# Block products in the second group, weight sums on GpSimd, state products between blocks: a fused scan and feed-forward kernel on one core

**Chip, cores, metric.** One core of one Trainium2 chip. The metric is the device time of one execution in microseconds. All times compared here are of fast runs; a core alone has no second die to compare with, so a run counts as slow only where it is over 1.5% above the fastest of its kernel.

## The reference, cut to what matters

```python
# state-space scan: batch 4, 8 heads, 768 steps, head 32, state 16, chunks of 32
for c in range(nc):
    cum = np.cumsum(log_a_chunk, axis=-1)
    L = np.exp(cum[:, :, :, None] - cum[:, :, None, :]) * causal
    y = einsum((Cc @ Bc^T) * L, xc) + (Cc @ state) * exp(cum)     # ... cut
    state = exp(sum(log_a_chunk)) * state + sum(Bc x xc * decay)  # ... cut
# feed-forward on all 3072 tokens, 256 -> 2048 -> 256
h = x @ w_in
g = h * (1.0 / (1.0 + np.exp(-1.702 * h)))
return g @ w_out
```

All is float32. The kernel takes chunks of 128 steps and the tokens in six groups of 512; a group is two pairs of chunks. While group g goes through the two big products, the state work of group g+1 is done.

## The kernel before

The feed-forward has 8 blocks of hidden units a group. A block's product, cut into 2 x 2 parts, takes 8 part products in the plain way or 7 by the known trick of mixing the parts with sums beforehand and afterwards. Mixing the weights costs 32 sums, once for the whole kernel:

```python
def mix_in(n):                                   # n = 0..3, for blocks 2n, 2n+1 of the first product
    ...
    for o, u, v, op in ((s1, a21, a22, ALU.add), (s2, s1, a11, ALU.subtract),
                        (s3, a11, a21, ALU.subtract), (s4, a12, s2, ALU.subtract)):
        nc.vector.tensor_tensor(out=o, in0=u, in1=v, op=op)   # 128 x 256, float32
    ...
def mix_w(n): ...                                # the same for the second product's weights
def mix_y(g): ...                                # three sums that mix the group's input yT
```

`hidden(g, f)` is half a plain block: two matmuls of 512 columns (a matmul leaves two records in these traces: the 16 plain blocks of four matmuls are 128 records of L660). `first(g, j, i)` is one of the seven products of block j; the letters D, T, S in the order strings are the additions (VectorE) and Silu calls (ScalarE) that follow. `product(g, j)` is a block of the second product, by seven already. The state work of a pair p: `decay` (VectorE scans, L352, and Be, L397), `turn` (transposes), `advance` (TensorE A, then VectorE S: L582, L589), `score` (TensorE cb, L539), `weigh` (VectorE multiplies L by cb in PSUM, L550), `finish` (TensorE y, L607 and L616, then ScalarE copies into yT). The first group is all plain, groups 3 to 6 all by seven. The second group stands between them with an order of its own, plain in the first product:

```python
for step in "H0 H1 H2 H3 H4 P0 H5 P1 H6 P2 H7 P3 P4 P5".split():
    j = int(step[1:])
    if step[0] == "H":
        hidden(1, 2 * j)
        hidden(1, 2 * j + 1)
    else:
        product(1, j)
    for do in after.get(step, []):     # state work and sums, listed by step  ... cut
        do()
for g in range(2, NG):                 # the loop of the later groups  ... cut
```

Of the kernel before, what the change touches and what calls it, by code (L numbers as in the profile page):

```python
# [16 lines left out]
P = 128  # L17
# [18 lines left out]
def kernel(  # L36
# [444 lines left out]
    def turn(p):  # L481
        turn_only(p)
        since_start(p)
# [61 lines left out]
    def weigh(p, ks=(slice(0, 2),)):  # L545

        L, cb = Ls[p], st[p]["cb"]
        Lv = L.rearrange("p k r q i -> p k r (q i)")
        for k in ks:
            nc.vector.tensor_tensor(out=Lv[:, k], in0=Lv[:, k],  # L550
                                    in1=cb.rearrange("p r k e -> p k r e")[:, k], op=ALU.mult)
# [7 lines left out]
    def gain(p):  # L559
        b, c = divmod(2 * p, NC)  # L560
        Be = BE.pop(p)
        nk = 1 if c + 2 == NC else 2
        A = bank(f"A{p}")[:, :2 * Q * D].rearrange("p (k e) -> p k e", k=2)
        for k in range(nk):
            for r in range(R):
                heads = slice(Q * r, Q * r + Q)
                nc.tensor.matmul(out=A[32 * r:32 * r + 32, k],  # L567
                                 lhsT=Be[:, k, heads].rearrange("p h n -> p (h n)"),
                                 rhs=rx[p][:, k, heads].rearrange("p h d -> p (h d)"),
                                 start=True, stop=True, tile_position=(0, 32 * r),  # L570
                                 skip_group_check=True)
        increment[p] = A
# [20 lines left out]
    def finish(p, late=False):  # L593
        for part_of in finish_parts(p, late):
            part_of()
# [73 lines left out]
    def mix_in(n):  # L669

        t = wide.tile([P, PN], FP32, tag=("m", "p2")[n % 2], name=f"mi{n}").rearrange(
            "p (j s e) -> p j s e", j=2, s=4)
        w = w_in[:, :, 4 * n * P:4 * (n + 1) * P].rearrange(
            "p k (j i e) -> p k j i e", j=2, i=2)
        a11, a12, a21, a22 = w[:, 0, :, 0], w[:, 1, :, 0], w[:, 0, :, 1], w[:, 1, :, 1]
        s1, s2, s3, s4 = (t[:, :, i] for i in range(4))
        for o, u, v, op in ((s1, a21, a22, ALU.add), (s2, s1, a11, ALU.subtract),
                            (s3, a11, a21, ALU.subtract), (s4, a12, s2, ALU.subtract)):
            nc.vector.tensor_tensor(out=o, in0=u, in1=v, op=op)
        for k in range(2):  # L680
            mixed_in[2 * n + k] = t[:, k]

# [88 lines left out]
    def mix_w(n):  # L771

        if n % 2 == 0:
            mixed_w["tile"] = words(f"mw{n}").bitcast(FP32).rearrange(
                "p (n j s e) -> p n j s e", n=2, j=2, s=4)
        t = mixed_w["tile"][:, n % 2]
        w = w_out[:, 4 * n:4 * n + 4].rearrange("p (j i) (c e) -> p j i c e", i=2, c=2)
        a11, a12, a21, a22 = w[:, :, 0, 0], w[:, :, 1, 0], w[:, :, 0, 1], w[:, :, 1, 1]
        s1, s2, s3, s4 = (t[:, :, i] for i in range(4))
        for o, u, v, op in ((s1, a21, a22, ALU.add), (s2, s1, a11, ALU.subtract),  # L780
                            (s3, a11, a21, ALU.subtract), (s4, a12, s2, ALU.subtract)):
            nc.vector.tensor_tensor(out=o, in0=u, in1=v, op=op)
        for k in range(2):
            mixed_w[2 * n + k] = t[:, k]

# [173 lines left out]
    def at(places, i, *work):  # L959
        places.setdefault(i, []).extend(work)  # L960
# [24 lines left out]
    at(in_project[0], 7, lambda: turn(PG + 1))  # L985
    at(in_project[0], 9, lambda: narrow(9))
    at(in_project[0], 10, lambda: advance(PG + 1), lambda: scores(PG + 1))
    at(in_project[0], 14, lambda: finish(PG + 1))
    for i in range(4):
        at(in_project[0], 14, lambda i=i: mix_in(i))  # L990
    for k in range(PG):
        at(in_project[0], 8 + k, lambda k=k: load(2 * PG + k))
    for k, i in enumerate((9, 11, 13, 15)):
        at(in_project[0], i, lambda k=k: spread(2 * CG + k))


    after = {}
    n, p = 2 * PG, 3 * PG

    def late(p):  # L1000
        gain(p)
        keep(p)
        score(p)
        weigh(p)

    at(after, "H0", lambda: decay(2 * CG), lambda: decay(2 * CG + 1), lambda: turn(n))
    at(after, "H1", lambda: late(n), lambda: decay(2 * CG + 2), lambda: decay(2 * CG + 3),
       lambda: turn(n + 1))
    at(after, "H3", lambda: finish(n), lambda: load(p + 1), lambda: late(n + 1))
    at(after, "H4", lambda: finish(n + 1))  # L1010
    for k, i in enumerate(("H4", "P0", "P2", "P5")):
        at(after, i, lambda k=k: mix_w(k))
    for j in range(NF // 2):
        at(after, f"P{min(j - 1, 5)}" if j else "H4", lambda j=j: mix_g(1, j))
    for k in range(CG):
        at(after, f"P{k}", lambda k=k: decay(3 * CG + k))
        at(after, "H1" if k < 2 else "H3", lambda k=k: spread(3 * CG + k))
    at(after, "P3", lambda: clip_rows(2), lambda: decay_rows(2), lambda: turn(p))
    at(after, "P4", lambda: mix_y(2), lambda: advance(p), lambda: turn(p + 1))
    at(after, "P5", lambda: advance(p + 1))  # L1020
    assert [b for b in range(NB) if 3 * CG <= b * NC < 4 * CG] == [2]


    for f in range(NF):
# [1 line left out]
        for do in in_hidden[0].get(f, []):  # L1026
            do()
    project_all(0, in_project[0])
    load(p)
    spread_rows(2)  # L1030
    for step in "H0 H1 H2 H3 H4 P0 H5 P1 H6 P2 H7 P3 P4 P5".split():
        j = int(step[1:])
        if step[0] == "H":
            hidden(1, 2 * j)
            hidden(1, 2 * j + 1)
        else:
            product(1, j)
        for do in after.get(step, []):
            do()

    def run(g, steps, products=(), **do):

# [12 lines left out]
    def seven(g, j):  # L1055
        return [(g, j, (i,)) for i in ORDER]

    for g in range(2, NG):
        n, p = (g + 1) * PG, (g + 2) * PG
        more, most = g + 1 < NG, g + 2 < NG  # L1060
        chunks = list(range((g + 2) * CG, (g + 3) * CG)) if most else []
        rows = [b for b in range(NB) if most and (g + 2) * CG <= b * NC < (g + 3) * CG]
        if most:
            load(p)
            for c in chunks[:2]:
                spread(c)
            for b in rows:
                spread_rows(b)
        run(g, "0.1 P P 0.6 P P 0.7 P 0.5 P 0.2 P 0.D", seven(g - 1, 6))
        run(g, "1.1 0.S P 0.4 P P 1.6 P 0.3 0.T M P P 1.7 P 1.5 1.2 1.D C", seven(g - 1, 7),  # L1070
            M=lambda: mix_g(g, 0), C=lambda: combine(g - 1))
        if more:
            a, b = finish_parts(n), finish_parts(n + 1)
            run(g, "2.1 1.S 1.4 1.3 2.6 2.5 2.2 2.7 1.T s1 2.D 2.S w1 2.4 give 2.3 3.1 2.T s2 w2 3.6 "
                "y1 3.7 y2 y3 3.5 3.2 3.D", s1=lambda: score(n), w1=lambda: weigh(n), give=lambda: give(g - 1),
                s2=lambda: score(n + 1), w2=lambda: weigh(n + 1), y1=a[0], y2=a[1], y3=a[2])
            if most:
                load(p + 1)
                for c in chunks[2:]:
                    spread(c)  # L1080
            run(g, "P P 3.S 3.4 P P 3.3 3.T P P P M", seven(g, 0), M=lambda: mix_g(g, 1))
            for r in rows:
                clip_rows(r)
                decay_rows(r)
            run(g, "4.1 y1 4.6 4.5 y2 4.7 4.2 y3 4.D M", y1=b[0], y2=b[1], y3=b[2],
                M=lambda: mix_g(g, 2))
            if most:
                decay(chunks[0])
        else:
            run(g, "2.1 1.S 1.4 1.3 2.6 2.5 2.2 2.7 1.T 2.D 3.1 2.S 2.4 3.5 3.6 2.3 3.2 3.7 2.T 3.D M",  # L1090
                M=lambda: mix_g(g, 1))
        for j in range(5 if more else 4, NF // 2):
            h = "{1}.1 {0}.S P {0}.4 P {1}.6 P {0}.3 P {1}.7 {0}.T P {1}.5 P {1}.2 P {1}.D M".format(j - 1, j)
            run(g, h, seven(g, j - 4), M=lambda: mix_g(g, j - 2))
            if most:
                decay(chunks[j - 4])
        k = NF // 2 - 1
        run(g, f"P {k}.S P {k}.4 P P {k}.3 {k}.T P P P", seven(g, 4))
        if not more:
            give(g - 1)  # L1100
            for j in range(k - 1, k + 1):
                mix_g(g, j)
            break
        mix_g(g, 6)
        if most:
            turn(p)
        mix_y(g + 1)
        run(g, "P P A P T P P P P B", seven(g, 5),
            **{"A": lambda: most and advance(p), "T": lambda: most and turn(p + 1),
               "B": lambda: most and advance(p + 1)})  # L1110
        mix_g(g, 7)
# [33 lines left out]
```

## Time and profile before

| | before |
|---|---|
| median of the first runs | 383.5 us |
| span of the profiled run | 383.8 us |
| TensorE busy | 97% |
| chain of waits on TensorE | 95% |

The stage in which the change lies can be cut out by two instructions that all versions have: the scores of the second group's second pair (cb), and the first product X of group 3. From the first to the second I call it the stage. These are their rows in the TensorE timeline of the kernel before (start, length, engine, line, output and inputs, shapes, records):

```profile
79.38 1.15 PE L539 MATMUL cb<-CT,BT 32*128 32x256 f32 x16
...
147.75 0.70 PE L717 MATMUL X<-yT,w_in 128*128 128x256 f32 x2
```

The stage takes 147.75 - 79.38 = 68.37 us. From group 3's start it is another 231.7 us to the start of TensorE's last record. I call this the tail; in the traces below it is the same to 0.03 us, with two exceptions that are named where they come up.

The chain of waits before, by engine:

```profile
PE 95%; DVE 2%; DMA 1%; ACT 1%; issue 1%; ACTq 0%; DVEq 0%
```

### The profile page before, as it was taken

The numbers are of one execution on the slowest core, as the hardware profiler recorded it, in microseconds if no ns is written. First come the engines' busy times: TensorE is split into PE (matmuls) and PEld (weight loads), VectorE is DVE, ScalarE is ACT, GpSimd is POOL, SyncE is SP. The second block draws the span as 40 slices with busy tenths as digits, with TensorE's granted clock in tenths as the row PEclk, the third lists the DMA queues.
The fourth block names the chain that finished last, engine by engine and source line by source line (L and its number), as shares of the span: only waits on it lengthen the run. The fifth ranks groups of instructions, "written<-read, shape, count | busy, mean of one in ns | idle before, by whom it ended". The sixth has DMA issues, their size and how long they took to land.

```text
span 383.8 us, 5725 instructions
## 1 busy us (share of the span) xinstructions
PE 373.2 (97%) x2258; PEld 281.1 (73%) x2258; DVE 267.7 (70%) x438; ACT 152.0 (40%) x337; POOL 11.7 (3%) x34
## 2 busy tenths in 40 slices
PE   7979999999999999999999999999999999999995
PEld 3544447886556678877888867888877888888884
DVE  4589998999879968567787564879383446454353
ACT  3658836401432122553333453333453432453330
POOL 5210000000000010000000000000000000000000
PEclk9999999999999999999999999999999999999999
DMA  9998949442967110068200045000010000000011
GB/s 150 235 252 199 242 149 178 86 168 62 194 102 161 73 43 0 0 110 167 81 30 0 2 84 138 0 0 2 0 56 2 0 0 3 0 0 2 0 56 55
DMA packets 85794, 29.56 MB, mean 77 GB/s; under 512 B 75720, under 2 KB 79240, under 8 KB 85768
## 3 DMA queue, kind: packets, MB, share of 16 engines
q1 hardware_dynamic: 83592, 28.94, 32.4%
q10 hardware_dynamic: 2176, 0.26, 0.5%
q8 instruction: 18, 0.29, 0.3%
q14 instruction: 8, 0.07, 0.1%
HBM read 25.95 MB, written 3.24 MB: 76 GB/s over the span
## 4 chain that ended last, share of the span: by engine, by line
PE 95%; DVE 2%; DMA 1%; ACT 1%; issue 1%; ACTq 0%; DVEq 0%
PE acc L814 32%; PE X L717 16%; PE h L660 14%; PE Y L727 11%; PE o L757 7%; PE cb L539 3%; PE y L616 3%; PE ab L460 2%; PE tp L496 2%; PE y L607 2%; PE oT L848 1%; PE A L567 1%; DMA az<-in_a_dram 1%; DVE L L550 1%; ACT yT L638 0%
## 5 line engine op out<-in xcount | busy, mean ns | idle before, releaser
L814 PE MATMUL acc<-mg,mw 128*128 128x256 f32 x240 | 65.3, 379 | 0.0
L660 PE MATMUL h<-yT,w_in 128*128 128x512 f32 x128 | 56.9, 595 | 0.0
L722 ACT ACTIVATE ac<-X 128x256 f32<-128x256 f32 x64 | 24.6, 384 | 77.0 <-PE X L717 77.0
L831 DVE TENSOR_TENSOR gT<-Y,ac 128x512 f32<-128x512 f32 x32 | 22.1, 692 | 46.4 <-PE Y L727 44.4
L814 PEld LDWEIGHTS acc<-mg,mw 128*128 128x128 f32 x240 | 45.4, 190 | 6.1
L694 ACT ACTIVATE gT<-gT 128x512 f32<-128x512 f32 x64 | 33.3, 520 | 30.5 <-DVE gT L831 30.5
L660 PEld LDWEIGHTS h<-yT,w_in 128*128 128x128 f32 x128 | 23.9, 190 | 27.6 <-issue 25.7
L814 PE MATMUL acc<-gT,w_out 128*128 128x256 f32 x160 | 43.8, 380 | 0.0
L352 DVE TENSOR_TENSOR_SCAN L<-a,idents 128x1024 f32<-128x1024 f32 x18 | 41.1, 2283 | 0.0
L717 PE MATMUL X<-my,mi 128*128 128x256 f32 x128 | 39.3, 389 | 0.1
L663 ACT ACTIVATE gT<-h 128x512 f32<-128x512 f32 x32 | 19.0, 595 | 41.5 <-PE h L660 41.2
L814 PEld LDWEIGHTS acc<-gT,w_out 128*128 128x128 f32 x160 | 29.9, 190 | 5.3 <-issue 1.4
L831 DVE TENSOR_TENSOR gT<-Y,b 128x256 f32<-128x256 f32 x32 | 13.5, 421 | 29.0 <-PE Y L727 29.0
L550 DVE TENSOR_TENSOR L<-L,cb 128x2048 f32<-128x2048 f32 (+1 forms) x13 | 27.6, 2122 | 3.8 <-PE cb L539 3.7
L757 PE MATMUL o<-w_out,gT 128*128 128x256 f32 x128 | 29.3, 383 | 0.0
L685 DVE TENSOR_TENSOR mg<-gT 128x512 f32<-128x512 f32 x40 | 27.3, 684 | 1.9 <-ACT gT L694 1.9
L717 PEld LDWEIGHTS X<-my,mi 128*128 128x128 f32 x128 | 23.3, 190 | 5.3 <-ACT gT L694 1.0
L757 PEld LDWEIGHTS o<-w_out,gT 128*128 128x128 f32 x128 | 23.8, 190 | 4.1 <-issue 0.7
L814 PE MATMUL acc<-gT,mw 128*128 128x256 f32 x80 | 23.7, 382 | 0.0
L814 PE MATMUL acc<-mg,w_out 128*128 128x256 f32 x80 | 23.5, 379 | 0.0
L717 PE MATMUL X<-yT,w_in 128*128 128x256 f32 x64 | 19.7, 389 | 0.9 <-ACT yT L638 0.9
L722 ACT ACTIVATE b<-X 128x256 f32<-128x256 f32 x32 | 12.3, 384 | 19.8 <-PE X L717 19.7
(134 smaller groups left out, 522.2 us busy)
## 6 DMA issues: line engine op xcount, KB each, us to landing
a<-scratch SPq DMA_DIRECT2D x18, 512.0 KB, 5.6
bits<-in_moe_w_out_dram SPq DMA_DIRECT2D x4, 1024.0 KB, 7.1
x<-in_x_dram SPq DMA_DIRECT2D x24, 128.0 KB, 3.4
out_dram<-ob SPq DMA_DIRECT2D x11, 256.0 KB, 2.2
bits<-in_moe_w_in_dram SPq DMA_DIRECT2D x4, 512.0 KB
bits<-in_moe_w_in_dram SPq DMA_DIRECT2D x2, 1024.0 KB
b<-in_B_dram SPq DMA_DIRECT2D x24, 64.0 KB, 3.9
c<-in_C_dram SPq DMA_DIRECT2D x22, 64.0 KB, 2.7
```

The lines of the kernel that those rows point to most:

```text
L352: nc.vector.tensor_tensor_scan(out=Ls[p][:, k].rearrange("p r q i -> p (r q i)"), data0=ra[n], data1=idents.rearrange("p h i -> p (h i)"), ...
L550: nc.vector.tensor_tensor(out=Lv[:, k], in0=Lv[:, k], in1=cb.rearrange("p r k e -> p k r e")[:, k], op=ALU.mult)
L660: nc.tensor.matmul(out=h, lhsT=w_in[:, k, f * P:(f + 1) * P], rhs=yT[g][:, k], start=(k == 0), stop=(k == NK - 1))
L663: nc.scalar.activation(gT[g, j][:, i], h, AF.Silu, scale=GELU_SCALE)
L685: nc.vector.tensor_tensor(out=t[:, 0:2], in0=B[:, :, 1], in1=B[:, 0], op=ALU.subtract)
L694: nc.scalar.activation(o, i, AF.Silu, scale=GELU_SCALE)
L717: nc.tensor.matmul(out=s["X"], lhsT=lhsT, rhs=rhs, start=i == "1", stop=i == "4", skip_group_check=True)
L722: nc.scalar.activation(copy, s["X"], AF.Copy)
L727: nc.tensor.matmul(out=o, lhsT=lhsT, rhs=rhs, start=s.pop("new", False), stop=i != "5", skip_group_check=True)
L757: nc.tensor.matmul(out=o[k // 2][:, k % 2], lhsT=gT[g, f // 2][:, f % 2, k * P:(k + 1) * P], rhs=w_out[:, f], start=(f == 0 and k % 2 == 0 ...
L814: nc.tensor.matmul(out=acc[g][0][i], lhsT=lhsT, rhs=rhs, start=(j == 0 and i in (0, 2, 5, 6)), stop=(j == NF // 2 - 1), skip_group_check=True)
L831: nc.vector.tensor_tensor(out=o, in0=v, in1=w, op=ALU.add)
```

## The change

Its intent: give the second group the cheaper seven products from block 3 on, take the 32 weight sums off VectorE, the second busiest engine, and lay the state's output products between running blocks as the later groups do. The diff in full:

```diff
--- before.py
+++ after.py
@@ -676,7 +676,7 @@
         s1, s2, s3, s4 = (t[:, :, i] for i in range(4))
         for o, u, v, op in ((s1, a21, a22, ALU.add), (s2, s1, a11, ALU.subtract),
                             (s3, a11, a21, ALU.subtract), (s4, a12, s2, ALU.subtract)):
-            nc.vector.tensor_tensor(out=o, in0=u, in1=v, op=op)
+            nc.gpsimd.tensor_tensor(out=o, in0=u, in1=v, op=op)
         for k in range(2):
             mixed_in[2 * n + k] = t[:, k]
 
@@ -779,7 +779,7 @@
         s1, s2, s3, s4 = (t[:, :, i] for i in range(4))
         for o, u, v, op in ((s1, a21, a22, ALU.add), (s2, s1, a11, ALU.subtract),
                             (s3, a11, a21, ALU.subtract), (s4, a12, s2, ALU.subtract)):
-            nc.vector.tensor_tensor(out=o, in0=u, in1=v, op=op)
+            nc.gpsimd.tensor_tensor(out=o, in0=u, in1=v, op=op)
         for k in range(2):
             mixed_w[2 * n + k] = t[:, k]
 
@@ -985,40 +985,17 @@
     at(in_project[0], 7, lambda: turn(PG + 1))
     at(in_project[0], 9, lambda: narrow(9))
     at(in_project[0], 10, lambda: advance(PG + 1), lambda: scores(PG + 1))
-    at(in_project[0], 14, lambda: finish(PG + 1))
-    for i in range(4):
-        at(in_project[0], 14, lambda i=i: mix_in(i))
+    at(in_project[0], 13, lambda: finish(PG + 1))
+    for i in (1, 2):
+        at(in_project[0], 13, lambda i=i: mix_in(i))
+    at(in_project[0], 13, lambda: decay(2 * CG))
+    at(in_project[0], 14, lambda: decay(2 * CG + 1), lambda: turn(2 * PG))
+    for i in range(2):
+        at(in_project[0], 14, lambda i=i: mix_w(i))
     for k in range(PG):
         at(in_project[0], 8 + k, lambda k=k: load(2 * PG + k))
-    for k, i in enumerate((9, 11, 13, 15)):
+    for k, i in enumerate((7, 7, 9, 9)):
         at(in_project[0], i, lambda k=k: spread(2 * CG + k))
-
-
-    after = {}
-    n, p = 2 * PG, 3 * PG
-
-    def late(p):
-        gain(p)
-        keep(p)
-        score(p)
-        weigh(p)
-
-    at(after, "H0", lambda: decay(2 * CG), lambda: decay(2 * CG + 1), lambda: turn(n))
-    at(after, "H1", lambda: late(n), lambda: decay(2 * CG + 2), lambda: decay(2 * CG + 3),
-       lambda: turn(n + 1))
-    at(after, "H3", lambda: finish(n), lambda: load(p + 1), lambda: late(n + 1))
-    at(after, "H4", lambda: finish(n + 1))
-    for k, i in enumerate(("H4", "P0", "P2", "P5")):
-        at(after, i, lambda k=k: mix_w(k))
-    for j in range(NF // 2):
-        at(after, f"P{min(j - 1, 5)}" if j else "H4", lambda j=j: mix_g(1, j))
-    for k in range(CG):
-        at(after, f"P{k}", lambda k=k: decay(3 * CG + k))
-        at(after, "H1" if k < 2 else "H3", lambda k=k: spread(3 * CG + k))
-    at(after, "P3", lambda: clip_rows(2), lambda: decay_rows(2), lambda: turn(p))
-    at(after, "P4", lambda: mix_y(2), lambda: advance(p), lambda: turn(p + 1))
-    at(after, "P5", lambda: advance(p + 1))
-    assert [b for b in range(NB) if 3 * CG <= b * NC < 4 * CG] == [2]
 
 
     for f in range(NF):
@@ -1026,17 +1003,6 @@
         for do in in_hidden[0].get(f, []):
             do()
     project_all(0, in_project[0])
-    load(p)
-    spread_rows(2)
-    for step in "H0 H1 H2 H3 H4 P0 H5 P1 H6 P2 H7 P3 P4 P5".split():
-        j = int(step[1:])
-        if step[0] == "H":
-            hidden(1, 2 * j)
-            hidden(1, 2 * j + 1)
-        else:
-            product(1, j)
-        for do in after.get(step, []):
-            do()
 
     def run(g, steps, products=(), **do):
 
@@ -1055,7 +1021,7 @@
     def seven(g, j):
         return [(g, j, (i,)) for i in ORDER]
 
-    for g in range(2, NG):
+    for g in range(1, NG):
         n, p = (g + 1) * PG, (g + 2) * PG
         more, most = g + 1 < NG, g + 2 < NG
         chunks = list(range((g + 2) * CG, (g + 3) * CG)) if most else []
@@ -1066,14 +1032,38 @@
                 spread(c)
             for b in rows:
                 spread_rows(b)
-        run(g, "0.1 P P 0.6 P P 0.7 P 0.5 P 0.2 P 0.D", seven(g - 1, 6))
-        run(g, "1.1 0.S P 0.4 P P 1.6 P 0.3 0.T M P P 1.7 P 1.5 1.2 1.D C", seven(g - 1, 7),
-            M=lambda: mix_g(g, 0), C=lambda: combine(g - 1))
+        if g == 1:
+            mix_in(3)
+            mix_w(2)
+            mix_w(3)
+            mix_in(0)
+            decay(2 * CG + 2)
+            hidden(g, 0)
+            hidden(g, 1)
+            advance(n)
+            decay(2 * CG + 3)
+            hidden(g, 2)
+            scores(n)
+            hidden(g, 3)
+            turn(n + 1)
+            hidden(g, 4)
+            advance(n + 1)
+            scores(n + 1)
+            mix_y(g)
+            mix_g(g, 0)
+            hidden(g, 5)
+        else:
+            run(g, "0.1 P P 0.6 P P 0.7 P 0.5 P 0.2 P 0.D", seven(g - 1, 6))
+            run(g, "1.1 0.S P 0.4 P P 1.6 P 0.3 0.T M P P 1.7 P 1.5 1.2 1.D C", seven(g - 1, 7),
+                M=lambda: mix_g(g, 0), C=lambda: combine(g - 1))
         if more:
-            a, b = finish_parts(n), finish_parts(n + 1)
-            run(g, "2.1 1.S 1.4 1.3 2.6 2.5 2.2 2.7 1.T s1 2.D 2.S w1 2.4 give 2.3 3.1 2.T s2 w2 3.6 "
-                "y1 3.7 y2 y3 3.5 3.2 3.D", s1=lambda: score(n), w1=lambda: weigh(n), give=lambda: give(g - 1),
-                s2=lambda: score(n + 1), w2=lambda: weigh(n + 1), y1=a[0], y2=a[1], y3=a[2])
+            ya, yb = finish_parts(n), finish_parts(n + 1)
+            if g == 1:
+                run(g, "3.1 y1 3.6 y2 3.7 y3 3.5 3.2 3.D", y1=ya[0], y2=ya[1], y3=ya[2])
+            else:
+                run(g, "2.1 1.S 1.4 1.3 2.6 2.5 2.2 2.7 1.T s1 2.D 2.S w1 2.4 give 2.3 3.1 2.T s2 w2 3.6 "
+                    "y1 3.7 y2 y3 3.5 3.2 3.D", s1=lambda: score(n), w1=lambda: weigh(n), give=lambda: give(g - 1),
+                    s2=lambda: score(n + 1), w2=lambda: weigh(n + 1), y1=ya[0], y2=ya[1], y3=ya[2])
             if most:
                 load(p + 1)
                 for c in chunks[2:]:
@@ -1082,7 +1072,7 @@
             for r in rows:
                 clip_rows(r)
                 decay_rows(r)
-            run(g, "4.1 y1 4.6 4.5 y2 4.7 4.2 y3 4.D M", y1=b[0], y2=b[1], y3=b[2],
+            run(g, "4.1 y1 4.6 4.5 y2 4.7 4.2 y3 4.D M", y1=yb[0], y2=yb[1], y3=yb[2],
                 M=lambda: mix_g(g, 2))
             if most:
                 decay(chunks[0])
```

## The prediction

The recorded texts speak of a lock. The word is the author's name for a slowdown: in the trace before, L589 takes 0.75 us beside a GpSimd sum and 0.35 us with GpSimd idle (rows at 19.59 and 25.16 us). Its size, 0.6 us a sum, is the author's estimate from these rows; that the two engines take strict turns is an assumption of the layout in part (4). What lies behind the slowdown, no run here shows.

> **What bounds the kernel now.** I read the page first (busy shares, the 40 slices, the chain of waits), then the chain in order of time from 90 to 180 us, then VectorE and GpSimd in order of time.
>
> ```profile
> PE 373.2 (97%) x2258; PEld 281.1 (73%) x2258; DVE 267.7 (70%) x438; ACT 152.0 (40%) x337; POOL 11.7 (3%) x34
> ...
> PE   7979999999999999999999999999999999999995
> ...
> DVE  4589998999879968567787564879383446454353
> ```
>
> TensorE is busy 97% of the span and 9 tenths in nearly every slice after the start; the clock row is 9 throughout. So the time is the sum of TensorE's work plus a few waits, and a change pays only by shortening TensorE's work or by opening or closing waits. VectorE is close behind in the slices of 50 to 130 us, the stretch that the change touches. GpSimd is free there.
>
> The stage in question is the second group's, from 92.6 us (its first product starts) to 147.8 us (group 3's starts): 55.2 us. In the chain, in order of time (start, length, what, records):
>
> ```profile
> 108.91 1.05 PE y L607 x8
> ...
> 115.79 0.65 PE y L607 x8
> 116.44 1.01 PE y L616 x32
> 117.45 3.22 PE acc L814 x14
> 120.67 3.43 PE h L660 x8
> 124.10 3.02 PE acc L814 x14
> ```
>
> A plain block of the first product (two hidden tiles) is 8 records, 3.43 us. A block by seven products is 14 records; the second product has that form already and takes 3.02 us. After the small products of the state (L607, L616) the first big product is 0.2 us longer (3.22 for 3.02): the switch between small and full tiles. The first L607 group takes 1.05 where the second takes 0.65: 0.4 us of waiting. There is hardly another gap in the stage; at most about half a microsecond of waits can be recovered.
>
> [...] Rows of the two engines in order of time (start, length, engine, line, output and inputs):
>
> ```profile
> 5.45 1.44 POOL L334 COPY idents<-ident 128x1024 f32<-128x1024 f32 x1
> 19.47 0.73 POOL L524 TENSOR_TENSOR CsT<-C,since 128x256 f32<-128x256 f32 x1 [5.52 <-ACT C L501]
> ...
> 5.15 2.29 DVE L292 TENSOR_TENSOR_SCAN cum<-carry,cum 128x256 f32<-128x256 f32 x2 [0.48 <-ACT cum L287]
> ...
> 19.59 0.75 DVE L589 SCALAR_TENSOR_TENSOR S<-S,since 128x128 f32<-128x128 f32 x1
> 25.16 0.35 DVE L589 SCALAR_TENSOR_TENSOR S<-S,since 128x128 f32<-128x128 f32 x1
> ```
>
> L589 takes 0.35 us at 25.16 with GpSimd idle, but 0.75 beside a GpSimd sum: it starts at 19.59 and ends at 20.34, so its work began near 20.0, when the sum that began at 19.47 let go. The sum therefore holds the lock about 0.6 us. The two scans of 256 end only at 7.44, because the copy (to 6.89) stands between them[...].
>
> [...] The trace: 0.73 us for 256 elements on GpSimd[...], against 0.42 on VectorE:
>
> ```profile
> L679 DVE TENSOR_TENSOR mi<-w_in 128x256 f32<-128x256 f32 x8 | 3.4, 420 | 0.0
> L782 DVE TENSOR_TENSOR mw<-w_out 128x256 f32<-128x256 f32 x8 | 3.3, 418 | 0.0
> ```
>
> **The change part by part.**
>
> (1) Seven products from block 3: blocks 3 to 7, so 5 x (3.43 - 3.02) = -2.05 us of TensorE. All of it is on the path.
>
> (2) State products between blocks. Before, one pair's output products cost 0.65 + 1.01 + one switch 0.2 = 1.86 us. In the general loop they come in three parts; group 3 shows the form:
>
> ```profile
> 175.52 0.65 PE y L607 x8
> 176.16 0.63 PE X L717 x2
> ...
> 177.23 0.57 PE y L616 x16
> 177.80 0.63 PE X L717 x2
> ```
>
> Here X is 0.63 instead of its usual 0.43 after each part. So 0.65 + 2 x 0.57 + 3 x 0.2 = 2.39, that is +0.53 a pair, +1.06 for two pairs. The last part is followed in group 3 by 0.28 us of idle time for the copy into yT (page of waits: X from yT); one such is added, +0.3. The scores and state updates of the next group now stand alone between hidden tiles, two more switches: +0.3. The 0.4 us at the first L607 goes: -0.4.
>
> (3) The second group's own mixed inputs (mix_y, L685 to L687: 0.68 + 0.43 + 0.43, about 1.5 us on VectorE) must end, at least their second sum, before block 3's second product. VectorE comes to them after weighing the second pair's scores (2.3 us), just as the last plain block ends: I estimate 0.5 us of waiting even without the lock.
>
> Sum without contention: -2.05 + 1.06 + 0.3 + 0.3 - 0.4 + 0.5 = -0.3 us. The block form's gain is nearly eaten by switches.
>
> (4) The sums. 32 sums leave VectorE: back to back they start every 0.34 to 0.46 us, mean 0.36, so -11.5 us of VectorE. Added to it: 5 blocks x (0.69 + 0.42 for the additions L831) = 5.6, and 1.5 for mix_y; net -4.4 us. On GpSimd they are 32 x about 0.68 = 22 us, with 32 x 0.6 = 19 us of lock. GpSimd is idle and runs ahead, so I expect it to begin as soon as its earlier instructions are through, near 77 us, and to end between 110 and 116 us. In that time VectorE is nearly always running something: scans (2.28 us, two SBUF inputs), joins of the last weights (1.2 us), Be[...]. I laid the two queues out alternating, turn by turn, with these durations, and TensorE's order beside them. These waits came of it: 0.5 us for the last piece of w_out, whose join ends at 82.5 before and is needed at 84.1; 0.9 for the weighing of the second group's second pair, before its output products (which are moved one step earlier); 0.5 + 1.9 for the scores of the next group's second pair, because the first pair's weighing is late (scans and state updates each lost 0.6 us several times); 1.2 more at mix_y. Together +5.0 us. VectorE's lag at the end of the stage goes into group 3, where it is busy only 43 of 59 us, so no more comes later.
>
> **Rivals.** A: the lock works as laid out: -0.3 + 5.0 = +4.7, 388.2 us. For it: the rows at 5 and 19 us. Against: the layout assumes strict turns and that the sums start at 77[...]. B: contention is hidden, because VectorE runs ahead: the decays of the next group are now issued before the first stage ends (85 instead of 93 us), which gives up to 8 us of lead; then -0.3 to +1, 383 to 384.5 us. Speaking for it: the sums leave VectorE 4.4 us lighter. C: VectorE falls so far behind that the second product's mixed inputs come late too, block after block: 391 to 394 us; unlikely, as from block 3 on the sums are nearly over. D: the pure gain of part (1), 381.4; it would need that inserted products cost no switch, which group 3 contradicts.
>
> **Range and chances.** A 0.5, B 0.4, C 0.07, D 0.03: 0.5 x 388.2 + 0.4 x 383.8 + 0.07 x 392.5 + 0.03 x 381.4 = 386.5 us. Eight in ten: 382.3 to 390.6. Two per cent is 7.7 us: slower than 391.1 only in C, 0.07; faster than 375.8 would need more than all of part (1), 0.01.
>
> **What would show it.** L660 falls from 128 to 88 records, X and Y at L717 and L727 rise by 70; the spacing of block 3's products is 0.43 and 0.63 next to state products. GpSimd's busy time rises by about 20 us, as 32 sums of 0.7 us or, where they waited, up to 3 us. Scans beside them last over 2.3 us. The waits of TensorE name cb, y or X at VectorE between 84 and 115 us if A holds, and do not if B does. The prediction is wrong if scans keep 2.28 us beside GpSimd's sums, if the sums start only at 90 us, or if new waits stand after 125 us.

## The result

The changed kernel took 388.31 us in the median of 4 runs (387.19 to 388.77), the kernel before 383.55 (383.42 to 385.18). The ratio is 1.011, with a 95% interval of 1.0074 to 1.0145. Ratios here are the mean time of one kernel's fast runs over that of the other's of the same rounds, so not quite the ratio of the medians quoted.

From the page of the changed kernel, the lines that answer to those of before (busy time by engine, 40 slices), and the chain's shares by engine:

```profile
PE 372.5 (96%) x2288; PEld 285.7 (74%) x2288; DVE 270.0 (70%) x419; ACT 157.7 (41%) x357; POOL 46.7 (12%) x66
...
POOL 5210000099971000000000000000000000000000
...
PE 83%; DVE 13%; issue 2%; DMA 1%; ACT 1%; ACTq 0%; POOL 0%; DVEq 0%; POOLq 0%
```

TensorE has less work (372.5 for 373.2 us), yet the span is 3.3 us longer. GpSimd's 9s stand in slices 9 to 11, a 7 in slice 12 (77 to 116 us). Most telling is the chain: VectorE's share of it rose to 13% (before it was 2%). A stretch that TensorE bounded is now bounded by VectorE. (The granted clock is 1.00 in both traces in every stretch from 44 to 150 us, so the clock is not the cause.) The chain in order of time shows which (start, length, what):

```profile
85.05 2.28 DVE L L550
87.33 2.68 DVE L L352
...
90.59 2.84 DVE L L352
...
103.92 2.27 DVE L L550
...
110.96 0.84 DVE my L686
111.94 0.67 PE X L717 x2
```

From 85 to 112 us the chain lies on VectorE. The page of waits of TensorE (us in all, times, longest), where the kernel before has the first of these with 1.5 us in two waits and neither of the others:

```profile
PE y L616 <- DVE L L550: 2.0, 3, 1.1
PE X L717 <- DVE my L686: 1.5, 1, 1.5
...
PE cb L539 <- DVE L L550: 1.0, 1, 1.0
```

And the rows of VectorE and GpSimd in order of time, beside each other:

```profile
87.25 2.75 DVE L352 TENSOR_TENSOR_SCAN L<-a,idents 128x1024 f32<-128x1024 f32 x1
90.03 0.64 DVE L397 TENSOR_TENSOR Be<-b,L 128x128 f32<-128x128 f32 x1
...
103.92 2.27 DVE L550 TENSOR_TENSOR L<-L,cb 128x2048 f32<-128x2048 f32 x1
...
77.03 0.73 POOL L679 TENSOR_TENSOR mi<-w_in 128x256 f32<-128x256 f32 x1
...
87.93 2.59 POOL L782 TENSOR_TENSOR mw<-mw,w_out 128x256 f32<-128x256 f32 x1
...
104.67 0.72 POOL L782 TENSOR_TENSOR mw<-mw,w_out 128x256 f32<-128x256 f32 x1
```

The scan of two SBUF inputs takes 2.75 us for 2.28, Be 0.64 for 0.29, and the sum that meets the scan takes 2.59 for 0.73. The weighing L550, one of whose inputs is in PSUM, keeps its 2.27 us, and the sum beside it keeps its 0.72. That is the slowdown which the prediction calls the lock, and the weighing shows none of it. The two rows that bound the stage:

```profile
79.65 1.15 PE L539 MATMUL cb<-CT,BT 32*128 32x256 f32 x16
...
151.03 0.70 PE L717 MATMUL X<-yT,w_in 128*128 128x256 f32 x2
```

The stage takes 151.03 - 79.65 = 71.38 us, 3.01 more than before. What lies ahead of it adds 0.27 to the profiled span, the tail nothing.

### The profile page after: what moved, and what is told of

The parts are those of the page before. It is cut to its first block, busy times and chain, and to the rows that moved or that the text cites. A ratio compares the mean times of both kernels' runs of the same rounds, so it can differ in the third digit from the quotient of the medians.

```text
span 387.1 us, 5829 instructions
## 1 busy us (share of the span) xinstructions
PE 372.5 (96%) x2288; PEld 285.7 (74%) x2288; DVE 270.0 (70%) x419; ACT 157.7 (41%) x357; POOL 46.7 (12%) x66
## 4 chain that ended last, share of the span: by engine, by line
PE 83%; DVE 13%; issue 2%; DMA 1%; ACT 1%; ACTq 0%; POOL 0%; DVEq 0%; POOLq 0%
PE acc L814 31%; PE X L717 18%; PE Y L727 13%; PE h L660 7%; DVE L L352 3%; DVE L L550 3%; PE cb L539 2%; PE y L616 2%; PE ab L460 2%; PE o L757 2%; PE oT L848 1%; PE tp L496 1%; PE y L607 1%; DVE p L184 1%; DMA az<-in_a_dram 1%
## 5 line engine op out<-in xcount | busy, mean ns | idle before, releaser
L722 ACT ACTIVATE ac<-X 128x256 f32<-128x256 f32 x74 | 28.3, 383 | 86.8 <-PE X L717 86.8
L831 DVE TENSOR_TENSOR gT<-Y,ac 128x512 f32<-128x512 f32 x37 | 25.6, 691 | 52.3 <-PE Y L727 50.2
L694 ACT ACTIVATE gT<-gT 128x512 f32<-128x512 f32 x74 | 38.5, 520 | 38.5 <-DVE gT L831 38.5
L717 PE MATMUL X<-my,mi 128*128 128x256 f32 x148 | 45.6, 390 | 1.6 <-DVE my L686 1.5
L352 DVE TENSOR_TENSOR_SCAN L<-a,idents 128x1024 f32<-128x1024 f32 x18 | 43.2, 2397 | 0.0
L660 PE MATMUL h<-yT,w_in 128*128 128x512 f32 x88 | 39.6, 598 | 0.0
L717 PEld LDWEIGHTS X<-my,mi 128*128 128x128 f32 x148 | 26.8, 189 | 7.8 <-POOL mi L679 1.6
L660 PEld LDWEIGHTS h<-yT,w_in 128*128 128x128 f32 x88 | 16.2, 190 | 19.3 <-issue 17.3
L550 DVE TENSOR_TENSOR L<-L,cb 128x2048 f32<-128x2048 f32 (+1 forms) x13 | 27.5, 2118 | 3.4 <-PE cb L539 3.3
L717 PE MATMUL X<-yT,w_in 128*128 128x256 f32 x74 | 22.7, 389 | 1.1 <-ACT yT L638 1.1
L663 ACT ACTIVATE gT<-h 128x512 f32<-128x512 f32 x22 | 13.1, 594 | 23.5 <-PE h L660 23.2
```

What stands on the lines that cost most here:

```text
L352: nc.vector.tensor_tensor_scan(out=Ls[p][:, k].rearrange("p r q i -> p (r q i)"), data0=ra[n], data1=idents.rearrange("p h i -> p (h i)"), ...
L550: nc.vector.tensor_tensor(out=Lv[:, k], in0=Lv[:, k], in1=cb.rearrange("p r k e -> p k r e")[:, k], op=ALU.mult)
L660: nc.tensor.matmul(out=h, lhsT=w_in[:, k, f * P:(f + 1) * P], rhs=yT[g][:, k], start=(k == 0), stop=(k == NK - 1))
L663: nc.scalar.activation(gT[g, j][:, i], h, AF.Silu, scale=GELU_SCALE)
L694: nc.scalar.activation(o, i, AF.Silu, scale=GELU_SCALE)
L717: nc.tensor.matmul(out=s["X"], lhsT=lhsT, rhs=rhs, start=i == "1", stop=i == "4", skip_group_check=True)
```

## The experiments

All experiments ran with five rounds beside the kernel before (medians 385.0 to 385.2 us on those chips; the fast runs of one kernel scatter over 2 us and more, which is why I lean on the stage in the traces as well). The stage, as defined above, and the ratio:

| kernel | stage us | against before | ratio of times (95%) |
|---|---|---|---|
| before | 68.37 | | |
| changed, again | 71.39 | +3.0 | 1.0077 (1.0056 to 1.0099) |
| sums as memsets (wrong result) | 68.60 | +0.2 | 1.0005 (0.9990 to 1.0020) |
| sums on VectorE | 78.44 | +10.1 | 1.0247 (1.0224 to 1.0271) |
| before, sums on GpSimd | 69.94 | +1.6 | 1.0035 (1.0014 to 1.0055) |
| held back | 69.50 | +1.1 | 1.0036 (1.0012 to 1.0060) |
| held back, unsplit | 69.22 | +0.9 | 1.0029 (1.0012 to 1.0046) |
| sums twice | 90.21 | +21.8 | 1.0550 (1.0526 to 1.0573) |
| hybrid | none | | 1.0188 (1.0142 to 1.0234) |
| hybrid, other order | 73.76 | +5.4 | 1.0151 (1.0106 to 1.0196) |
| staged | 69.56 | +1.2 | 1.0029 (1.0011 to 1.0047) |
| staged, last sums moved | 67.18 | -1.2 | 0.9975 (0.9956 to 0.9994) |

One per cent is 3.85 us; read so, the ratios follow the stage to within 0.7 us in every row that has one. The stage is where the time goes. In two traces the tail is longer as well: by 0.9 us in the hybrid's other order (0.6 of it a wait for mixed weights at 155 us) and by 0.3 in the last kernel of the table (a wait at 334 us, of which I can't say that the edit made it). Each stage is that of one traced run. The waits of 0.35, 0.4, 0.7, 0.8, 1.6 and 1.8 us given below are read from the spacing of TensorE's starts; the page of waits has less (0.2 for 0.35, 1.1 for 1.6, 1.7 for 1.8).

### The changed kernel again

No edit.

> The changed kernel unaltered, as the yardstick of its call. Theory[...]: again about 1.1% over the kernel before (some 4 us), with the same four waits of TensorE in the trace: output products of the second group's second pair 0.6 us, scores of the next group's second pair 1.0 us, block 3's second product 1.5 us. Rival (start-up or granted clock makes the difference): the excess varies from run to run with the clock and the stage between the first product of group 2 and that of group 3 is the same length as before.

The same waits stood in the trace, the stage was 71.39 us, and the ratio 1.0077 is 3.0 us. So the 4.2 us of the first comparison hold some 1.2 us that are not in the stage; both intervals contain 1.0077. The changed kernel's fast runs have nearly the same mean in both comparisons (388.1 and 388.0 us); that of the kernel before is 383.9 in the first and 385.0 in the second. Three of its four first runs lie between 383.4 and 383.7, where only 9 of the 42 fast ones of the second comparison lie below 384. So most of the remainder is which runs of the kernel before were drawn; why it has these faster runs stays open.

### The lock taken away: sums as memsets

```diff
-            nc.gpsimd.tensor_tensor(out=o, in0=u, in1=v, op=op)
+            nc.gpsimd.memset(o, 0.0)
```

> Wrong result on purpose: each GpSimd sum becomes a memset of the same tile, which reads no SBUF, so the order and every dependency stay[...]. Lock theory: scans beside it take 2.28 us again, the three waits shrink to nothing except about 0.5 us at block 3's second product, and the time falls by 2.5 to 3.5 us, to within 1 us of the kernel before. Rival (the new order of the second group, its switches and VectorE's program order cost the time whatever GpSimd does): stays within 1 us of the changed kernel, about 387 to 388 us.

The result is wrong on purpose (relative error 1.16). Every order and dependency stays. VectorE's and GpSimd's rows in order of time:

```profile
85.04 2.28 DVE L352 TENSOR_TENSOR_SCAN L<-a,idents 128x1024 f32<-128x1024 f32 x1
...
83.19 2.04 POOL L782 MEMSET mw<- 128x256 f32 x8
85.17 1.05 POOL L679 MEMSET mi<- 128x256 f32 x4
```

Four memsets lie inside the scan, and it keeps 2.28 us. Of the new waits only 0.6 us at L686 is left, and the stage is 68.60. So with the sums gone, the new order of the second group is worth +0.23 us, and the sums cost 71.38 - 68.60 = 2.78. A memset is also shorter than a sum (0.26 for 0.7 us), so this run alone does not tell the lock from the mere amount of GpSimd work; the held-back kernels do.

### The sums back on VectorE

```diff
-            nc.gpsimd.tensor_tensor(out=o, in0=u, in1=v, op=op)
+            nc.vector.tensor_tensor(out=o, in0=u, in1=v, op=op)
```

> The changed order with the 32 sums back on VectorE: no lock, but 11.5 us more of work in VectorE's queue ahead of the next group's scans. If the sums on GpSimd were simply a mistake, this is faster than the changed kernel, near 384 us. My own layout says it is slower still: VectorE reaches the state update of the next group about 5 us late, 389 to 393 us.

394.72 us, beyond the expected 393. Without the lock, but with the sums in VectorE's queue right ahead of the scans, TensorE waits 5.1 us at one place (rows of the TensorE timeline):

```profile
111.69 2.09 PE L539 MATMUL cb<-CT,BT 32*128 32x256 f32 x16 [5.10 <-DVE L L550]
113.71 3.44 PE L660 MATMUL h<-yT,w_in 128*128 128x512 f32 x4
```

After the wait the scores take 2.09 us, not 1.15, and four records of L660 take 3.44, where four take 1.98 in the changed kernel: TensorE runs at half pace for five microseconds (granted clock 0.53 from 111.5 to 117). This surcharge I had not counted. So in this order GpSimd is the better place for the sums in spite of the lock.

### The kernel before with only the sums moved

```diff
-            nc.vector.tensor_tensor(out=o, in0=u, in1=v, op=op)
+            nc.gpsimd.tensor_tensor(out=o, in0=u, in1=v, op=op)
```

> The kernel before with only the sums moved to GpSimd. Lock theory: scans beside them lengthen to about 2.8 us and TensorE waits at the next group's pairs; VectorE is at the same time 11.5 us lighter, so the net is small, +0.5 to +3 us on the kernel before. Rival (moving work off VectorE pays, since it was the second busiest engine): 383 us or less.

+1.3 us by the ratio and +1.6 in the stage, as the theory had it; the wait at the first y products grew from 0.4 to 1.6 us. To lighten the second busiest engine by 11.5 us of sums did not pay even in the old order (its busy time, lock included, fell only from 267.7 to 261.2 us).

### The same sums at other hours: held back

A small GpSimd copy that reads a tile of VectorE's holds GpSimd's queue until that tile is written (in the trace the two copies ran at 81.17 and 109.14 us, after GpSimd had been idle for 6.01 and 18.15 us until VectorE wrote S and mg):

```diff
-    for i in (1, 2):
-        at(in_project[0], 13, lambda i=i: mix_in(i))
+    turnstile = const.tile([P, 2], FP32, name="turnstile")
+    def hold(k, t):
+        nc.gpsimd.tensor_copy(turnstile[:, k:k + 1], t)
+    at(in_project[0], 13, lambda: hold(0, state[PG + 1][:, 0, 0:1]), lambda: mix_in(1))
 ...  mix_w(0) stays; after mix_g(1, 0):
+            hold(1, mixed_g[g, 0][:, 3, 0:1])
+            mix_in(2)
 ...  after the row decays: mix_w(1), mix_in(3), mix_w(2), mix_w(3), mix_in(0)
```

> The changed kernel with GpSimd's sums held back: the first input sums start only once the state of the second group's second pair is written (about 85 us), the second input sums only after the first mixed block (about 114 us), the rest after the row decays (about 121 us). Same sums, same lock, other hours. Lock theory: only 8 sums are left in the critical stretch, the three waits shrink to about 0.5 us in all, and the time comes within 1 us of the kernel before, like the memset kernel. Rival (it is the amount of GpSimd work beside VectorE, whenever it runs): stays at about 1% over the kernel before.

The waits at the second pair's y and at cb are gone, and the one at L686 is 0.6 us (page of waits):

```profile
PE X L717 <- DVE my L686: 0.6, 1, 0.6
```

The stage falls from 71.38 to 69.50. It is the same number of sums, on the same engine, with a lock as before (sums that met a scan still took 2.6 and 2.7 us): only their hours changed, and two tiny copies came in. That speaks against the amount of work as the cause. Two smaller waits of about 0.35 us came at 133 and 140 us, where the late sums now run beside scans, so the lever was not used up.

### Held back, with the state products in one run

```diff
-                run(g, "3.1 y1 3.6 y2 3.7 y3 3.5 3.2 3.D", ...
+                run(g, "3.1 y1 y2 y3 3.6 3.7 3.5 3.2 3.D", ...
-            run(g, "4.1 y1 4.6 4.5 y2 4.7 4.2 y3 4.D M", ...        # second group only
+            run(g, "4.1 y1 y2 y3 4.6 4.5 4.7 4.2 4.D M", ...
```

> The held-back sums, and in the second group the output products of a state pair in one run instead of three parts. By the switch cost of 0.2 us an insertion, four insertions fewer save 0.8 us, and the products fill the wait at block 3: 0.8 to 1.5 us under the held-back kernel, and some 0.5 to 1.5 us under the kernel before. Rival (switches are absorbed elsewhere): equal to the held-back kernel.

A miss: 69.22 against 69.50, less than the 0.8 us expected. The y products were shorter as computed, but ScalarE's copy of X now queued behind its copies into yT (a new wait of 0.7 us at 109.6), and the late sums left another of 0.7 at 134 us.

### Every sum twice

```diff
+            nc.gpsimd.tensor_tensor(out=o, in0=u, in1=v, op=op)
             nc.gpsimd.tensor_tensor(out=o, in0=u, in1=v, op=op)
```

> The changed kernel with every GpSimd sum done twice. Lock theory: up to 113 us GpSimd is already always waiting or running, so the three waits do not grow; the added sums run on to about 150 us and meet a VectorE with slack, so 0 to 2 us over the changed kernel. Rival (the loss is in proportion to the GpSimd work): another 3 to 4 us.

A plain miss, some 18 us over the changed kernel (405.8 for 388.0; 21 over the kernel before) instead of 0 to 2, and instructive, as neither theory had it. A row of VectorE's timeline:

```profile
140.56 1.76 DVE L419 TENSOR_TENSOR_SCAN since<-af,first 128x768 f32<-128x768 f32 x1 [20.73 <-POOL af L412]
```

The row decays of the next batch need two small instructions of GpSimd (0.20 and 0.11 us), and these stood behind the sums in its queue until 140 us: the last sum ended at 139.42 us, they began at 140.16 and 140.41. VectorE waited 20.7 us, TensorE 18.2. Up to there the lock's waits had indeed not grown (that at cb even vanished). GpSimd, busy 12% of the span in the changed kernel and so free on the average, was not free for a short job behind a long queue.

### The hybrid, and its other order

The 12 early sums stay on GpSimd; the 20 late ones go to VectorE:

```diff
+                mix_w(1, nc.vector)          # after the row decays
+                if j == 5:
+                    mix_in(3, nc.vector)     # behind block 5's mixed sums and scan
+                elif j == 6:
+                    mix_w(2, nc.vector)
 ...  mix_w(3, nc.vector) at j == 7; mix_in(0, nc.vector) behind the third group's mixed input
```

The other order also puts the second group's state products in one run behind two products that need no mixed input, as in "Staged" below.

> As the held-back kernel, but of the 32 sums only the 12 that meet an idle or PSUM-reading VectorE stay on GpSimd; the 20 late ones go to VectorE, placed after the blocks' mixed sums. A sum costs VectorE 0.36 us of its own time and 0.6 us when GpSimd does it beside a two-input instruction, so VectorE gains 20 x 0.24 = 5 us in the stage's second half and the two waits of 0.35 us at 133 and 140 us go: 0.5 to 1 us under the held-back kernel, within 0.5 us of the kernel before. Rival (GpSimd's sums are free once VectorE has slack): equal to the held-back kernel or slower.

> The hybrid, with the state's output products of the second group in one run, and the two products that need no mixed input put ahead of them. Switches: four insertions fewer, 0.8 us; the waits for the mixed input (0.6 us) and the one behind the copies into yT (0.7 us, seen in the earlier unsplit kernel) go as well. Expected 1 to 2 us under the hybrid and 1 to 1.5 us under the kernel before. Rival (ScalarE's copies queue behind yT again): no better than the hybrid.

Both missed. (The 0.6 us in the first text is the estimate named ahead of the prediction; a meeting cost a scan of the changed kernel 0.47 to 0.55 us.) The other order did so through a placement of mine: `mix_in(3)` is needed by block 6, and I had put it behind two scans. The hybrid has the same placement, but its profiled run was a slow one (938 us) and its trace is not used, so for it this is inferred (its verdict is "unclear", its time about 7 us over the kernel before). The trace of the other order shows the wait (TensorE's timeline, then busy times by stretch with the granted clock as PEclk):

```profile
126.54 0.59 PE L814 MATMUL acc<-gT,w_out 128*128 128x256 f32 x2
130.86 1.19 PE L717 MATMUL X<-my,mi 128*128 128x256 f32 x2 [3.72 <-DVE mi L679]
```

```profile
130.80:136.30 5.50, 5.44 (x13) 4.40 (x14) 1.01 (x3) 1.07 (x3) 0.00 (x0) 0.50 0.49 160
136.30:146.00 9.70, 9.70 (x46) 8.50 (x45) 7.85 (x14) 3.23 (x8) 0.00 (x0) 0.98 0.01 3
```

A wait of 3.7 us, and then 5.5 us at a granted clock of 0.50: products start every 0.43 us instead of every 0.22. Waits of 3.7, 5.1 and 18 us were followed by a clock near half (0.50, 0.53 and 0.54 in the stretches of 5.5 to 6 us there), those of 1.0 and 1.5 us of the changed kernel were not (1.00); the lengths between were not examined. The half pace lasted about 5.8, 5.0 and 3.6 us, an estimate from the mean granted clocks of the stretches (0.50 to 136.3 us and 0.98 from there to 146 in the first). So these two runs say nothing on how VectorE and GpSimd should share the sums.

### Staged

All sums on GpSimd in four groups, two of them let loose just ahead of the weighings of PSUM, and the state products in one run behind a product that needs no mixed input:

```diff
+            hold(1, BE[n + 1][:, 1, 0, 0:1])       # ahead of the first weighing
+            mix_in(2)
+            hold(2, state[n + 1][:, 0, 0:1])       # ahead of the second
+            mix_in(3)
 ...  mix_w(1), mix_w(2) after mix_g(1, 0); mix_w(3), mix_in(0) after the row decays
-                run(g, "3.1 y1 3.6 y2 3.7 y3 3.5 3.2 3.D", ...
+                run(g, "3.1 3.2 y1 y2 y3 3.6 3.5", ...
+                    "P P 3.7 3.D P P 3.S 3.4 P 3.3 3.T P 4.1 P M"      # then product(1, 0) and 4.1
+                    "4.2 4.6 y1 y2 y3 4.5 4.7 4.D M"
```

> The changed kernel with all 32 sums on GpSimd, but let loose in four groups: after the state of the second group's second pair, ahead of each of the two weighings of the next group (VectorE reads PSUM there for 2.2 us, so three sums fit beside it free), after the first mixed block, and after the row decays; and the state's output products in one run behind a product that needs no mixed input. Lock theory: the waits of 0.6, 1.0 and 1.5 us of the changed kernel go, four switches (0.8 us) go; the stage is 67.5 to 68.5 us from the second pair's scores to the third group (before 68.4, changed 71.4), the time 0 to 1 us under the kernel before. Rival (some cost of the new order that is not the lock): stays 1 us or more over the kernel before.

The three waits went, but the stage was 69.56: the last eight sums, from 118 to 127 us, left waits of 0.8 and 1.8 us behind them. The stage and the time (1.1 us over the kernel before) both missed what was expected.

### Staged, with the last eight sums moved

```diff
+            hold(4, st[n]["CsT"][:, 0, 0:1])       # opened at 93 us in the trace
+            mix_in(0)
-                mix_w(3)                           # after the row decays
-                mix_in(0)
+            mix_w(3, nc.vector)                    # behind the third group's mixed input
```

> The staged kernel with its last eight sums moved once more. In its trace they ran from 118 to 127 us beside two-input instructions and left two new waits, 0.8 us at 120 and 1.8 us at 126 us. The four input sums go to 90 us, where VectorE idles or reads PSUM; the four output sums go to VectorE behind the third group's mixed input (1.5 us). Lock theory: both waits go, the stage falls from 69.6 to about 67 us (before 68.4), the time 1 to 1.5 us under the kernel before. Rival (VectorE simply has too much to do in the second half of the stage, whoever sums): a wait of over 1 us stays between 118 and 130 us.

Rows of VectorE and GpSimd beside each other, and the two rows that bound the stage:

```profile
101.05 2.28 DVE L550 TENSOR_TENSOR L<-L,cb 128x2048 f32<-128x2048 f32 x1
...
101.33 0.73 POOL L679 TENSOR_TENSOR mi<-w_in 128x256 f32<-128x256 f32 x1
102.14 0.73 POOL L679 TENSOR_TENSOR mi<-mi,w_in 128x256 f32<-128x256 f32 x1
102.83 0.73 POOL L679 TENSOR_TENSOR mi<-w_in 128x256 f32<-128x256 f32 x1
```

```profile
79.19 1.15 PE L539 MATMUL cb<-CT,BT 32*128 32x256 f32 x16
...
146.37 0.70 PE L717 MATMUL X<-yT,w_in 128*128 128x256 f32 x2
```

Three sums fit beside the weighing and neither engine is slowed. Only the last eight sums differ from the staged kernel, and the stage is 2.38 us shorter: 67.18 us, 1.2 under the kernel before, as expected. The tail is 0.3 longer, and the ratio 0.9975 (0.9956 to 0.9994) is 1 us. It is a correct kernel and the only one here that beats the kernel before, by a quarter of a per cent (384.44 us for 385.17 in the medians of the fast runs), far inside the 2% that would count as faster. Four of its sums are on VectorE, and its state products are in one run, so it is not a measure of the hours alone.

## Why the prediction was right

The time, 388.31, lies in the stated range, and the class (within 2%) was the one given 0.92. The single figure of 386.5 was a mean over the rivals; the traces show that it was rival A, and B, C and D are out.

- **The block products and the switches.** L660 fell from 128 to 88 records, as said. The sum without contention was put at -0.3 us; the memset kernel measures +0.23, half a microsecond off. In its trace the first pair's products between blocks add 2.40 us (106.67 to 111.86, less five products of 0.43 us and the wait of 0.64), where 2.39 was put: the switches are there.
- **The wait at the mixed input without the lock.** Put at 0.5 us, measured 0.6 with memsets and when held back.
- **The sums' hours.** "Near 77 us" was 77.03; "between 110 and 116" was 113.3. They started so early because little held them: the first came right behind GpSimd's own earlier instructions (76.72 and 76.97 us). No new wait stands after 125 us, and the tail is unchanged.
- **The lock.** The scans beside sums took up to 2.83 us. The four waits were where the layout had put them, but their sum was mis-sized: 5.0 us predicted, 2.78 measured. The terms: the last piece of w_out 0.5, measured about 0.2; the second pair's y 0.9, measured 0.64; the next group's second scores 0.5 + 1.9 = 2.4, measured 1.03 in one wait; the mixed input 1.2 more, measured 0.89 more (1.53 in all). (These are differences to the memset kernel, by the spacing of starts; they add up to 2.78.) The scores' term is the one that was far off. Its mechanism was right: the first pair's weighing began at 103.92 us, 3.1 us later in the stage than with memsets (100.18), but only 1.03 us of this reached TensorE. A meeting costs a scan 0.47 to 0.55 us, not 0.6; the rows at 19 us that the prediction reads give 0.52 already (20.34 - 0.35 - 19.47). Why the layout came out later than the chip is not on record.
- **The busy times were wrong.** GpSimd's was to rise by about 20 us and rose by 35.0, since sums that met scans left longer records (up to 2.73 us for 0.73). Not lengthened, a sum took 0.73 us on GpSimd for 0.42 on VectorE. VectorE's was to fall by 4.4. With memsets it fell by 4.9, to 262.8; in the changed kernel it rose by 2.3, to 270.0. The lock thus cost VectorE 7.2 us, of which 2.78 reached the path.
- **A coincidence to own.** Rival A came to 388.2, and the clock said 388.31. But A was +4.7 us, and the stage shows +3.0. The first comparison's other 1.2 us were not found again in the second one, which gave 1.0077. The 383.5 on which the prediction builds comes from the same low draw of the kernel before; on the 385.0 of the later rounds A would have said 389.7, and the changed kernel took 388.0 there.
- **What I did not foresee** was how much is in the hours: the same sums on the same engine cost 2.8 us, or about 0.9 when held back, by when they ran; and the last kernel of the table, with 28 of the 32 on GpSimd, has a single idle stretch of TensorE over 0.1 us left in the stage (0.12 at 122 us).

Left open: how VectorE and GpSimd would best share the late sums (the hybrids failed for another reason), and why some runs of the kernel before are nearly 2 us faster than the others.

## What to carry to other kernels

Work moved to an idle engine was not free here: where a sum of GpSimd met a scan of VectorE, both took longer (up to 2.83 us for 2.28 and 2.7 for 0.73), and 2.78 us of this reached the path. Look for the stretches in which the engine to be relieved waits or, as in the weighing here, reads PSUM (2.27 us with sums of 0.72 beside it), and tie the moved work to them with a data dependency: the first sum, which the program has behind the second pair's output products (86.33 us on TensorE), began at 77.03 us. Before a form with fewer products is taken up, count the switches that come with it: here five cheaper blocks saved 2.05 us by the prediction's sum, and with the rest of the new order the stage was 0.23 us longer than before even without the sums. And see which short jobs of the idle engine are on another's path before a long queue is put ahead of them (20.7 us of VectorE's waiting with every sum twice).
